# Eight output stores at the end of a fused linear-attention and MLP kernel, issued by SyncE instead of GpSimd and ScalarE

## The chip, the cores and the metric

The kernel runs on one core of one Trainium2 chip. The metric is the device time of one execution in microseconds. Before the change it was 406.97 us as the median of three runs (405.87, 406.97 and 407.54).

## What is computed

The kernel computes a residual sum of a linear-attention block and an MLP with squared ReLU, both on the layer-normalised input, for 2048 tokens of 512 channels, in float32:

```python
phi = lambda t: jnp.where(t > 0, t + 1, jnp.exp(t)) + 1e-6
q, k, v = split_heads(xn @ wqkv)             # 32 heads of 16
kv = einsum("bhsd,bhse->bhde", phi(k), v); z = einsum("bhsd->bhd", phi(k))
A = (phi(q) kv / (phi(q) z + 1e-6)) @ wo
h = xn @ w1 + b1                             # 512 x 1376
B = relu(h)**2 @ w2 + b2                     # 1376 x 512
out = x + A + B                              # xn = layernorm(x)
```

(The split into heads and the einsums are shortened here.)

## The kernel before

Tokens stand in four groups of 512 (`BT`); a group is four tiles of 128 rows. A float32 product is made of three passes over high and low parts (`PASSES`, line 134). A first phase goes over all tokens for keys and values; then the groups 3 and 2 are done up to their stores, and then the groups 1 and 0 (`t1`, `t2` in the last part of the code). Instructions are issued to each engine in the order in which the code stands (`manual_schedule`, line 75): each engine works through its own list in order, and waits at an instruction until what it needs is there. A DMA is such an instruction too: the engine that issues it waits first for the data, then hands the transfer over, and goes on.

The change is at the very end, in the second product of the groups 1 and 0. That product is made block by block: the rows are the two token groups (r = 0 is group 1, r = 1 is group 0), the columns the left and the right half of the 512 output channels (`LO`, `HI`). Seven products M1 to M7 on TensorE make the four blocks, in the tiles `res[r, half]`; each such tile starts as the residual input (`load_block`, line 1732) and gets its products by `into` (line 1767), as an accumulating DMA from GpSimd or as an addition on VectorE.

- Block (0,0) is stored by line 1947, block (1,1) by line 1971: four stores each, issued by SyncE. A store of a block (`store_block`, line 1738) is cut by channel group; each of the four moves 128 KB in pieces of 256 bytes.
- Block (0,1) lacks its last product. It goes by four stores of SyncE into a scratch tensor `rowsd` (line 1965), and comes back by one load of 512 KB, issued by GpSimd, with tokens on the partitions, as `rows` (line 1967).
- Block (1,0) is turned out of the bank `d` by VectorE (`M4t`, line 1973), added into `res10` (lines 1974 and 1773) and stored by line 1975.
- Last, TensorE makes the product M3 for group 1 in four banks `end`, one for each tile of 128 tokens (line 1980, by the helper at line 140). When a bank is done, VectorE adds it into `rows` (line 1982), and a store of 128 KB writes that tile's right half (line 1984).

The counters that the rows of the order below name (`DMAHW0` to `DMAHW7` for transfers of SyncE and ScalarE, `DMASW0` to `DMASW7` for those of GpSimd) count transfers that have landed; they are used in turn, and a DMA that takes a counter waits until the transfer that had it before has landed. At the end of the program (line 2008) SyncE waits for all counters, and then all engines meet.

Of the kernel before, what the change touches and what calls it, by code (L numbers as in the profile page):

```python
# [13 lines left out]
P = 128  # L14
# [4 lines left out]
def kernel(  # L19
# [30 lines left out]
    nc = tc.nc  # L50
    xf = x.rearrange("b s d -> (b s) d")
    of = out.rearrange("b s d -> (b s) d")
# [84 lines left out]
    def three(ps, a, b, first, last):  # L137

        for n, (u, v) in enumerate(PASSES):
            nc.tensor.matmul(ps, lhsT=a[u], rhs=b[v], start=first and n == 0, stop=last and n == 2)  # L140
# [440 lines left out]
    for k in range(1, NJ):  # L581
        rows = slice(32 * k, 32 * (k + 1))
# [3 lines left out]
    for i0 in range(0, NT, TB):  # L586
# [6 lines left out]
        if i0 < NPE:  # L593
            single = work.tile([P, 3, 512], F32, name=f"xg{i0}s", tag="r0")
            for k in range(3):
                i = i0 + k - 1
# [3 lines left out]
        for k in range(0, n, 2):  # L600
            i = i0 + TB - n + k
# [401 lines left out]
    LO, HI = slice(0, D // 2), slice(D // 2, D)  # L1003
# [185 lines left out]
    for p in range(NO + 1):  # L1189
        at_p = AT[p]  # L1190
        kind, k = order[p] if p < NO else ("", 0)
        fa, fb = 2 * k, 2 * k + 1

        was, k = order[p - 1] if p else ("", 0)
# [481 lines left out]
    def rights(name, part):  # L1676

        key, kind, r, at = RIGHT[name]
        if part == "q":
            return [[(m if kind == "m" else mt)[u][:, 2 * r + i, at] for u in range(2)] for i in range(2)]  # L1680
        return [part_at[key, k] for k in ((0, 1), (2, 3), (4,))[part]]
# [39 lines left out]
    def token_rows(r, half, g, x):  # L1721

        t = (t2 if r else t1) * BT
        return rows_of(x[t:t + BT, half * 256:(half + 1) * 256], g)

    def rows_of(x, g):
        return x.rearrange("(b r) (g c) -> g r b c", r=Q, g=NJ)[g]

    def res_rows(o, g):
        return o[Q * g:Q * (g + 1)].rearrange("p a n -> p (a n)").rearrange("p (b c) -> p b c", c=2 * Q)  # L1730
# [7 lines left out]
    def store_block(r, half, to=None, engs=(nc.sync,)):  # L1738
        for g in range(NJ):
            o = token_rows(r, half, g, of) if to is None else rows_of(to, g)  # L1740
            engs[g % len(engs)].dma_start(o, res_rows(res[r, half], g))
# [25 lines left out]
    def into(r, half, tiles, eng="dma"):  # L1767
        for u in range(2):
            o = res[r, half][:, u]
            if eng == "dma":  # L1770
                nc.gpsimd.dma_start(o, tiles[u], accum_op=OP.add)
            else:
                nc.vector.tensor_tensor(out=o, in0=tiles[u], in1=o, op=OP.add)
# [64 lines left out]
    for p in range(NO):  # L1838
        kind, k = order[p]
# [126 lines left out]
    rows = work.tile([P, TB, 256], F32, name="rows", tag="x1")  # L1966
# [5 lines left out]
    do(low, 2)  # L1972
    m4 = turned_out("M4", Dc)
    into(1, 0, m4, "dve")
    store_block(1, 0, engs=(nc.gpsimd,))
    for parts in ((0, 1), (2, "q")):
        chunks = [(a, b) for part in parts for a, b in zip(half_units["M3", part], rights("M3", part))]
        for k in range(TB):
            for n, (a, b) in enumerate(chunks):
                three(ends[k], [v[:, k * P:(k + 1) * P] for v in a], b, False, "q" in parts and n == len(chunks) - 1)  # L1980
            if "q" in parts:
                nc.vector.tensor_tensor(out=rows[:, k], in0=ends[k], in1=rows[:, k], op=OP.add)
                i = t1 * TB + k
                nc.scalar.dma_start(of[i * P:(i + 1) * P, HI], rows[:, k])


# [26 lines left out]
```

## Time and profile before

| what | value |
|---|---|
| runs shown | 405.87, 406.97, 407.54 us |
| the profiled execution's own time | 406.98 us |
| its span | 404.9 us |
| mean granted clock of TensorE | 0.996 |
| output stores of SyncE from `res` at line 1741 | 8, of 128 KB |
| output stores of GpSimd from `res10` | 4, of 128 KB |
| output stores of ScalarE from `rows` | 4, of 128 KB |
| software queue of GpSimd | 4016 packets, 9.45 MB, 12.7% of the DMA engines' span |
| hardware queue of SyncE | 73472 packets, 77.23 MB, 61.0% |
| hardware queue of ScalarE | 656 packets, 0.52 MB, 0.4% |

The span is what the profile covers, from the first instruction to the last; the time of the execution is 2.08 us longer. In the rows of the profile the engines are PE (TensorE; PEld is its weight load), DVE (VectorE), ACT (ScalarE), POOL (GpSimd) and SP (SyncE); a name with a q behind it (SPq, ACTq, POOLq) is the engine's instruction queue, where DMAs are issued and waits are held. Times are in us from the span's start.

### The profile page before, as it was taken

How to read it: one execution, taken by the hardware profiler on the slowest of the kernel's cores; microseconds unless marked ns; L12 is line 12 of the kernel's file. 1: busy time of each engine (PE TensorE's matmuls, PEld its weight loads, DVE VectorE, ACT ScalarE, POOL GpSimd, SP SyncE). 2: the span in 40 equal slices, each digit the busy share in tenths (PEclk: the TensorE clock that was granted, in tenths of full speed). 3: DMA queues.
4: the chain of work that ended last, by engine and by line, in shares of the span. 5: the costliest groups of instructions: out<-in, count | busy, mean ns of one | idle time of the engine just before them, and what ended most of it. 6: DMA issues, size and time to landing. Idle time of an engine off the chain costs nothing.

```text
span 404.9 us, 5834 instructions
## 1 busy us (share of the span) xinstructions
PE 395.6 (98%) x1940; PEld 327.1 (81%) x1940; DVE 318.4 (79%) x537; ACT 259.8 (64%) x434; POOL 66.0 (16%) x106
## 2 busy tenths in 40 slices
PE   8999999999999999999999999999999999999992
PEld 7788888888788888888878888888888788888892
DVE  5886667587898989988499997269999895987841
ACT  5677777556788689887727860565986784565400
POOL 5443333220410000030000300200000001231111
PEclk9999999999999999999999999999999999999998
DMA  7857647911698745799796974896796867999953
GB/s 212 279 164 228 210 155 208 259 29 26 235 358 285 274 150 184 264 285 334 237 410 207 188 206 137 290 291 196 222 287 196 295 202 157 218 182 195 181 121 91
DMA packets 78172, 87.55 MB, mean 216 GB/s; under 512 B 24256, under 2 KB 59200, under 8 KB 77376
## 3 DMA queue, kind: packets, MB, share of 16 engines
q1 hardware_dynamic: 73472, 77.23, 61.0%
q0 software_dynamic: 4016, 9.45, 12.7%
q10 hardware_dynamic: 656, 0.52, 0.4%
q8 instruction: 15, 0.25, 0.3%
q14 instruction: 13, 0.11, 0.1%
HBM read 52.05 MB, written 28.84 MB: 200 GB/s over the span
## 4 chain that ended last, share of the span: by engine, by line
PE 93%; issue 3%; DVE 1%; DMA 1%; POOL 0%; ACT 0%; POOLq 0%
PE b L528 22%; PE acc L140 19%; PE pk L384 11%; PE kx L404 11%; PE a L1697 7%; PE b_c L528 5%; PE b_a L528 4%; PE b L1697 2%; PE y L1697 2%; PE d L1697 2%; PE b_b L528 2%; PE pz L140 1%; PE acc L539 1%; DMA x<-in_A_x_dram 1%; PE b L140 1%
## 5 line engine op out<-in xcount | busy, mean ns | idle before, releaser
L140 PE MATMUL acc<-w2r,s 128*128 128x512 f32 x240 | 57.0, 391 | 0.0
L140 PEld LDWEIGHTS acc<-w2r,s 128*128 128x128 f32 x240 | 44.9, 188 | 9.9 <-issue 0.4
L404 PE MATMUL kx<-pk,tok 128*128 128x512 f32 x192 | 46.0, 390 | 0.0
L404 PEld LDWEIGHTS kx<-pk,tok 128*128 128x128 f32 x192 | 36.0, 188 | 7.6 <-ACT pk L121 0.2
L528 PE MATMUL b<-T,aop 128*128 128x512 f32 x168 | 41.8, 390 | 0.0
L528 PEld LDWEIGHTS b<-T,aop 128*128 128x128 f32 x168 | 31.4, 188 | 7.4 <-ACT t L121 0.8
L365 POOL TENSOR_TENSOR tok<-xp,tok 128x512 fp32r<-128x512 f32 x15 | 20.2, 1344 | 39.8 <-ACT tok L121 39.8
L1088 POOL DMA_DIRECT2D res<-in_B_b_dram x8 | 7.1, 1004 | 107.7 <-DVE S L766 59.5
L132 DVE TENSOR_TENSOR M<-h,M 128x1024 fp32r<-128x1024 f32 (+1 forms) x15 | 15.2, 1038 | 5.4 <-ACT M L121 5.4
L1630 POOL DMA_DIRECT2D h<-h x6 | 5.3, 924 | 85.5 <-issue 64.5
L121 ACT ACTIVATE T<-Tf 128x512 fp32r<-128x512 f32 x16 | 9.4, 623 | 15.0 <-DVE Tf L709 14.9
L528 PE MATMUL b<-xs0h,aop 128*128 128x512 f32 x56 | 18.6, 392 | 0.0
L121 ACT ACTIVATE M<-h 128x1024 fp32r<-128x1024 f32 (+1 forms) x15 | 13.2, 908 | 7.6 <-PE a L1697 2.8
L121 ACT ACTIVATE pk<-k 128x512 fp32r<-128x512 f32 x16 | 10.1, 630 | 9.1 <-DVE k L379 9.1
L375 ACT ACTIVATE k<-pk 128x512 f32<-128x512 f32 x16 | 9.4, 589 | 9.8 <-PE pk L384 9.8
L140 PE MATMUL acc<-mh,aTsr 128*128 128x512 f32 x48 | 15.6, 390 | 0.0
L392 DVE SCALAR_TENSOR_TENSOR pk<-k,pk 128x512 fp32r<-128x512 f32 x16 | 11.3, 708 | 4.3 <-ACT pk L121 3.4
L242 DVE BATCH_NORM_STATS2 st<-x 128x6 f32<-128x512 f32 x16 | 10.9, 684 | 4.2 <-DMA x<-in_A_x_dram 4.1
L132 DVE TENSOR_TENSOR w2r<-r,w2r 128x512 fp32r<-128x512 f32 (+2 forms) x20 | 13.7, 683 | 0.5 <-ACT w2r L121 0.4
L379 DVE SCALAR_TENSOR_TENSOR k<-pk,k 128x512 f32<-128x512 f32 x16 | 10.9, 679 | 3.4 <-ACT k L377 3.0
L384 PE MATMUL pk<-wkh,xs1h 128*128 128x512 f32 x32 | 12.7, 396 | 0.2 <-ACT xs1h L332 0.2
L384 PE MATMUL pk<-wkl,xs0h 128*128 128x512 f32 x32 | 12.5, 390 | 0.0
(399 smaller groups left out, 1065.4 us busy)
## 6 DMA issues: line engine op xcount, KB each, us to landing
r<-in_B_w_dram SPq DMA_DIRECT2D x26, 256.0 KB, 4.4
aop_0d<-aop SPq DMA_DIRECT2D x7, 512.0 KB, 4.3
aop_1d<-aop SPq DMA_DIRECT2D x7, 512.0 KB, 5.4
aop_2d<-aop SPq DMA_DIRECT2D x7, 512.0 KB, 5.7
via<-xp SPq DMA_DIRECT2D x5, 512.0 KB, 2.7
xg<-via SPq DMA_DIRECT2D x20, 128.0 KB, 2.8
xTd<-t SPq DMA_DIRECT2D x8, 256.0 KB, 4.0
x<-in_A_x_dram SPq DMA_DIRECT2D x4, 512.0 KB, 4.5
```

Of the source, the lines that this page charges most:

```text
L121: nc.scalar.activation(o, i, AF.Copy, bias=bias)
L132: nc.vector.tensor_tensor(out=l, in0=src, in1=f32(h), op=OP.subtract)
L140: nc.tensor.matmul(ps, lhsT=a[u], rhs=b[v], start=first and n == 0, stop=last and n == 2)
L242: nc.vector.bn_stats(st[:, k, :], xr[tiles[k]])
L365: ENG[el].tensor_tensor(out=l, in0=src, in1=f32(h), op=OP.subtract)
L375: nc.scalar.activation(p, ps, AF.Relu, scale=-1.0)
L379: nc.vector.scalar_tensor_tensor(p, ps, 0.0, p, op0=OP.max, op1=OP.add)
L384: nc.tensor.matmul(ps, lhsT=cols(i)[u][:, j, slot(i)], rhs=w[v][:, j, :], start=first and n == 0, stop=last and n == len(steps) - 1)
L392: nc.vector.scalar_tensor_tensor(pk[i][:, 1], p, 1e-6, f32(pk[i][:, 0]), op0=OP.add, op1=OP.subtract)
L404: nc.tensor.matmul(kxp[c], lhsT=tok[i][:, u, c * P:(c + 1) * P], rhs=pk[i][:, v], start=i == 0 and (u, v) == first, stop=i == NT - 1 and ( ...
L528: nc.tensor.matmul(ps, lhsT=a[u][:, j * P:(j + 1) * P], rhs=b[v][:, j, :], start=first and j == 0 and n == 0, stop=last and j == 1 and n == 2,
L1697: nc.tensor.matmul(ps[e], lhsT=w, rhs=a[v], start=first and c == n == 0, stop=False, skip_group_check=True)
```

## The change

Two lines change. The four stores of block (1,0) lose the argument that gave them to GpSimd, so they take the default of `store_block`, SyncE; the four stores of `rows` are issued by SyncE in place of ScalarE. No data, size, address or computation changes, and no line changes its place.

```diff
@@ -1972,7 +1972,7 @@
     do(low, 2)
     m4 = turned_out("M4", Dc)
     into(1, 0, m4, "dve")
-    store_block(1, 0, engs=(nc.gpsimd,))
+    store_block(1, 0)
     for parts in ((0, 1), (2, "q")):
@@ -1981,7 +1981,7 @@
             if "q" in parts:
                 nc.vector.tensor_tensor(out=rows[:, k], in0=ends[k], in1=rows[:, k], op=OP.add)
                 i = t1 * TB + k
-                nc.scalar.dma_start(of[i * P:(i + 1) * P, HI], rows[:, k])
+                nc.sync.dma_start(of[i * P:(i + 1) * P, HI], rows[:, k])
```

SyncE's list at its end, with what each DMA waits for (`res_3537` is block (1,1), `res_3450` block (1,0), a minus is before and a plus after the change):

```order
 L1741 DMA out_dram<-res_3537 32x16x64 [waits DMAHW6_49]
-L1741 DMA out_dram<-res_3537 32x16x64 [waits DMAHW1_49]
-L1741 DMA out_dram<-res_3537 32x16x64 [waits DMAHW4_49]
+L1741 DMA out_dram<-res_3537 32x16x64 [waits DMAHW7_49]
+L1741 DMA out_dram<-res_3537 32x16x64 [waits DMAHW0_49]
+L1741 DMA out_dram<-res_3450 32x16x64 [waits DMAHW1_49,DVE_49]
+L1741 DMA out_dram<-res_3450 32x16x64 [waits DMAHW2_49]
+L1741 DMA out_dram<-res_3450 32x16x64 [waits DMAHW3_49]
+L1741 DMA out_dram<-res_3450 32x16x64 [waits DMAHW4_49]
+L1984 DMA out_dram<-rows 128x256 [waits DMAHW5_49,DMASW0_49,DVE_49]
+L1984 DMA out_dram<-rows 128x256 [waits DMAHW6_49,DVE_49]
+L1984 DMA out_dram<-rows 128x256 [waits DMAHW7_49,DVE_49]
```

The row of the fourth store of `rows` reads like the last one, with `DMAHW0`. SyncE gets eight DMAs behind its former last one, and the last two stores of block (1,1) take other counters.

GpSimd's list at its end, where `rows<-rowsd` is the load of the scratch tensor:

```order
 L1771 DMA res_3537<-Yt_3652 128x512 [waits DVE_49]
 L1967 DMA rows<-rowsd 128x4x256 [waits DMAHW2_49,DMAHW3_49,DMAHW1_49,DMAHW4_49,DMASW0_49,Activation_49]
-L1741 DMA out_dram<-res_3450 32x16x64 [waits DMASW1_49,DVE_49]
-L1741 DMA out_dram<-res_3450 32x16x64 [waits DMASW2_49]
-L1741 DMA out_dram<-res_3450 32x16x64 [waits DMASW3_49]
-L1741 DMA out_dram<-res_3450 32x16x64 [waits DMASW4_49]
 L2008 UNCONDITIONAL_BRANCH
```

The load of `rows` becomes GpSimd's last DMA, and it is issued behind the same waits.

ScalarE's list at its end, behind its last two copies:

```order
 L121 ACTIVATE M_3749<-h_2667 128x512 [waits DMASW0_49]
 L121 ACTIVATE M_q<-q_2571 128x1024 [waits DMASW1_49,DVE_49,PE_49]
-L1984 DMA out_dram<-rows 128x256 [waits DMAHW7_49,DMASW0_49,DVE_49]
-L1984 DMA out_dram<-rows 128x256 [waits DMAHW0_49,DVE_49]
-L1984 DMA out_dram<-rows 128x256 [waits DMAHW2_49,DVE_49]
-L1984 DMA out_dram<-rows 128x256 [waits DMAHW3_49,DVE_49]
 L2008 UNCONDITIONAL_BRANCH
```

Nothing stood behind these stores on ScalarE but the end of the program. TensorE's and VectorE's lists are unchanged.

## The prediction

> **What bounds the kernel now.** I read the page first, for the engine that fills the span, then the chain of waits over the last 30 us, since the change touches only the end of the program.
>
> ```profile
> span 404.9 us, 5834 instructions
> PE 395.6 (98%) x1940; PEld 327.1 (81%) x1940; DVE 318.4 (79%) x537; ACT 259.8 (64%) x434; POOL 66.0 (16%) x106
> PE   8999999999999999999999999999999999999992
> ```
>
> TensorE is busy for 98% of the span, in every one of the 40 slices but the last, where it is busy for two tenths. A slice is 404.9/40 = 10.1 us, so some 8 us at the end run without TensorE. That is the stretch in which the moved stores lie. The chain of waits, with start, length and holder:
>
> ```profile
> 374.73 9.54 PE d L1697 x42
> ...
> 386.52 1.44 DVE M4t L1762 x4
> 387.96 1.19 DVE res L1773 x2
> 389.15 2.93 issue
> 392.08 0.69 POOL out_dram L1741
> 392.76 2.19 issue
> 394.95 0.66 POOL out_dram L1741
> 395.62 2.71 issue
> 398.32 0.65 POOL out_dram L1741
> 398.97 2.15 issue
> 401.12 0.68 POOLq L2008
> ```
>
> The chain leaves TensorE when bank `d` is done, passes VectorE's turning and adding of block (1,0), and from 389.15 to the end it is GpSimd alone: four stores, each with 0.65 to 0.69 us of its own and 2.2 to 2.9 us of "issue" ahead of it, a time in which GpSimd waits for nothing that the profile shows. The data of all four were there at 389.15, yet the last store was issued only at 401.14. Its start to start distances are 2.87, 3.37 and 2.82 us. The other work of this stretch, from the timeline:
>
> ```profile
> 383.76 3.14 SPq L1741 DMA_DIRECT2D out_dram<-res  x4
> 387.33 0.80 POOL L1967 DMA_DIRECT2D rows<-rowsd  x1 [10.03 <-DMA rowsd<-res]
> 392.08 0.69 POOL L1741 DMA_DIRECT2D out_dram<-res  x1 [3.95 <-issue]
> 394.38 3.52 ACTq L1984 DMA_DIRECT2D out_dram<-rows  x4
> 396.79 0.28 PE L140 MATMUL end<-mh,M_q 128*128 128x256 f32 x1
> 397.11 0.42 DVE L1982 TENSOR_TENSOR rows<-end,rows 128x256 f32<-128x256 f32 x1 [0.64 <-PE end L140]
> 401.14 0.66 POOL L1741 DMA_DIRECT2D out_dram<-res  x1 [2.17 <-issue]
> ```
>
> TensorE ends at 397.07, VectorE's fourth addition at 397.53, and ScalarE's fourth store is issued at once: the four take 394.38 to 397.90, with 0.34 us for the last, so it starts at 397.56. SyncE has issued its last DMA by 386.90. So the end is bound neither by TensorE nor by the transfers themselves but by how slowly GpSimd puts out four stores. The windows of 1 us show this from the DMA side (the last two numbers are the busy share of the 16 DMA engines, and GB/s):
>
> ```profile
> 392.00:393.00 1.00, 1.00 (x10) 1.00 (x10) 0.00 (x0) 0.00 (x0) 0.69 (x1) 1.00 0.00 0
> 393.00:394.00 1.00, 1.00 (x11) 1.00 (x10) 0.07 (x1) 0.00 (x0) 0.00 (x0) 1.00 0.75 131
> 401.00:402.00 1.00, 0.00 (x0) 0.00 (x0) 0.00 (x0) 0.00 (x0) 0.66 (x1) 0.75 0.00 0
> 402.00:403.00 1.00, 0.00 (x0) 0.00 (x0) 0.00 (x0) 0.00 (x0) 0.00 (x0) 0.50 0.75 131
> ```
>
> One store of 128 KB keeps the DMA engines busy for about 0.75 us, and they stand idle between two of them.
>
> **The change part by part.** First, the four stores of block (1,0). What goes is GpSimd's tail from 389.15. What comes is four issues on SyncE, which can start when the additions end, at 389.15 + 0.03. How long SyncE takes for such stores, and how long they and the other transfers need from issue to landing:
>
> ```profile
> L1741 SPq DMA_DIRECT2D out_dram<-res x8: 316/567/1593, 377.8 to 386.6; - x8
> DMA to landing us min/median/max: 2.3/2.9/3.9
> ...
> rows<-rowsd POOLq DMA_DIRECT2D x1, 512.0 KB, 4.4
> out_dram<-res POOLq DMA_DIRECT2D x1, 128.0 KB, 2.5
> out_dram<-rows ACTq DMA_DIRECT2D x1, 128.0 KB, 1.7
> ...
> DMA to landing us min/median/max: 1.7/1.9/2.9
> ```
>
> (The first two rows are those of line 1741, the landing over all its stores; the next two are the load of `rows` and GpSimd's last store, then ScalarE's last store alone, and the last row is that of all four stores of line 1984.) Four stores of the same form took SyncE 3.14 us above, so the last is issued by about 392.3, and with the longest landing of 3.9 us it has landed by 396.2. That lies beside TensorE's last product, which runs to 397.07: it costs nothing. If that cover were gone, these stores would still end 7.4 us earlier than GpSimd's last did (401.14 + 2.5 = 403.64).
>
> The counters cost nothing either. The four new stores take `DMAHW1` to `DMAHW4`, last held by the four stores into `rowsd`; GpSimd's load at 387.33 waited for just these, so they had landed. The stores of `rows` take the counters of block (1,1), whose last issue was at 386.6 and landed by 386.6 + 3.9 = 390.5 at worst, ahead of the first addition's end at 394.35. The two stores of block (1,1) that change counters now wait for stores of block (0,0), which went out ahead of those into `rowsd`; should that cost some tenths, SyncE's idle time from 386.90 to 389.15 covers it.
>
> Second, the four stores of `rows`. They are queued behind block (1,0) on SyncE, done by 392.3, and the first is due at 394.38, so SyncE stands waiting for VectorE as ScalarE did. The last starts at 397.56 as before. What a store of this form takes from SyncE to landing the trace doesn't show; the same transfer from ScalarE took 1.7 us with nothing beside it, and 2.9 at worst, when GpSimd's stores ran beside it. SyncE's own stores, of 256-byte pieces, took 2.3 to 3.9. I take 1.7, since it is the same transfer and at 397.56 nothing else is left to move, and keep 1.7 to 2.9.
>
> Third, traffic: the new stores meet the load of `rows`, which landed at 387.33 + 4.4 = 391.7. The first addition needs it at 393.93, so there are 2.2 us to spare, and since the four additions take 4 x 0.42 = 1.7 us together, the last one would be late only if the load landed after 397.53 - 1.7 = 395.8, 4.1 us later than it did. I cost this at nothing; four stores at 0.75 us of engine time make 3.0 us in all.
>
> Fourth, the end of the program. SyncE waits there for the counters in turn:
>
> ```profile
> SPq L2008 <- DMA out_dram<-res: 5.3, 1, 5.3
> ...
> L2008 SPq DRAIN x3: 7/7/7, 404.1 to 404.4; - x3
> L2008 POOLq DRAIN x3: 46/98/2639, 401.1 to 404.7; - x3
> ```
>
> Its last long wait, 5.3 us, was for GpSimd's stores. From the last landing (403.64) to the span's end (404.9) are 1.26 us, of which the part behind SyncE's drain at 404.1 is 0.8 and the rest goes over counters that had long landed. I keep the 1.26 us, and take 0.46 us less as the low end. GpSimd's drain, 2.64 us from 401.1, moves ahead to its load of `rows` and is hidden.
>
> **The sum.** The new last landing is 397.56 + 1.7 = 399.26, in place of 403.64; with 1.26 us behind it the span ends at 400.5 in place of 404.9, 4.4 us earlier. Against the profiled execution's 406.98, which agrees with the median of the runs (406.97), this is **402.6 us**, 1.1% faster. What is late next is TensorE's last product: from there on, VectorE's addition, one store and the program's end follow in a chain that nothing else shares.
>
> The Trainium skill ("DMA: Bandwidth & Descriptors", section "Issuing engines are not separate DMA queues") says that DMAs of the scalar, sync and gpsimd engines run on the same 16 DMA engines, and that issuing from several only saves issue time, "usually small relative to the DMA itself". By that rule alone this change would move little. The trace differs for GpSimd: 2.8 to 3.4 us from issue to issue against 0.75 us of DMA time.
>
> **The rivals.** The first, on the other side: **SyncE's single list becomes the bound**. Eight stores now go through one engine in order, and an issue can be slow: 1.59 us was the longest of its block stores above, and elsewhere in the trace
>
> ```profile
> 360.00 11.69 SPq L1736 DMA_DIRECT2D res<-in_A_x_dram  x12
> 204.02 6.67 SPq L1121 DMA_DIRECT2D w2sd<-w2t  x3
> ```
>
> The loads of the blocks took 0.97 us each with the DMA engines full, the larger stores of line 1121 2.2 us each. With x us per issue the eighth starts at 389.18 + 7x. The forecast holds while that is ahead of 397.56, x up to 1.20; the end is where it was when it reaches 403.64 - 1.7 = 401.94, x = 1.82; beyond that the change is slower. At 2.2 the eighth starts at 404.6, the span ends at 404.6 + 1.7 + 1.26 = 407.5, and the time is **409.6 us**. Against it: stores of the same size and form took 0.67 to 0.79 us each, and four of the eight are spread by VectorE over 3.2 us. A case between, all at 1.59, puts the eighth at 400.3 and gives **405.4 us**, within 0.5%.
>
> The Trainium skill ("Perfetto Trace Analysis", section "DMA Optimizations") advises to balance DMAs across sync, scalar and GPSIMD where descriptor generation is the bottleneck; this change takes them together on one, and by that page it would be this rival. The trace bears it out only for GpSimd, the engine that it empties.
>
> Second: **the last store lands slower from SyncE**, with the block's stores still draining ahead of it on the same queue. At the 2.9 us of the worst store of `rows` the end moves by 1.2, to **403.8 us**. For it: SyncE's own rows have 2.3 as their least. Against: these are 512 pieces of 256 bytes each, and the block's stores should have landed 1.4 us ahead.
>
> Third: **the change doesn't shorten the end**, since the load of `rows` is held up by the new stores until about 400.2; the additions then end at 401.9, the last store lands at 403.6, and the time stays at **407.0 us**. That asks for 8.5 us of delay from four stores of 0.75 us.
>
> **How the numbers follow.** A measurement of this kernel can tell about 0.5% (2.03 us) from no change, so faster means below 404.9. The forecast has 0.84, the slower landing 0.08, the case between on SyncE's list 0.03, the held load 0.02, and SyncE's list as the bound, with more than 409.0, 0.03. The first two are faster, 0.92, and a part of the case between adds 0.02: 0.94. Within 0.5% lie the rest of it and the held load, 0.03. The range goes from the forecast less the 0.46 us at the end and about half the spread of the runs shown (407.54 - 405.87 = 1.67, half 0.8, of which I take 0.5), 401.6, up to the slower landing with the same 0.5, 404.3.
>
> **What would show it.** In the changed kernel's chain of waits no row of GpSimd should stand behind the load of `rows`; the end should read TensorE `end`, VectorE `rows`, SyncE's store of line 1984. SyncE's four stores of block (1,0) should start at about 389.2 and take 2.6 to 3.2 us; its last store should start 0.03 us behind VectorE's last addition, at about 397.6, and land 1.7 us later; from TensorE's last matmul to the span's end, 404.9 - 397.07 = 7.8 us before, there should be 3.4 us. The forecast is wrong if SyncE's issues take over 1.2 us each, if the additions wait for the load of `rows` in place of TensorE, or if the program's end has a part that GpSimd's stores had covered.

## The result, and the profile after

The changed kernel took 403.31 us as the median of five runs (402.91 to 403.62), against 406.97 us (405.87 to 407.92) for the kernel before: 3.7 us less, a ratio of 0.9908 with a 95% interval of 0.9888 to 0.9929. The forecast was 402.6 us, the range 401.6 to 404.3. The profiled execution has a span of 401.2 us in place of 404.9.

The page of the changed kernel, with the same rows as before and the queues of GpSimd (q0) and ScalarE (q10):

```profile
span 401.2 us, 5834 instructions
PE 395.2 (98%) x1940; PEld 326.6 (81%) x1940; DVE 318.1 (79%) x537; ACT 259.6 (65%) x434; POOL 63.0 (16%) x102
PE   7999999999999999999999999999999999999996
q0 software_dynamic: 3824, 8.92, 12.7%
q10 hardware_dynamic: 80, 0.00, 0.0%
```

TensorE's busy time is nearly what it was, 395.2 us in place of 395.6; what went is time without it, and the last slice shows six tenths in place of two. ScalarE's queue has lost its 0.52 MB, and GpSimd's 0.53 MB. The chain of waits at the end:

```profile
375.00 9.52 PE d L1697 x42
...
387.34 10.01 PE end L140 x84
397.35 0.02 issue
397.37 0.42 DVE rows L1982
```

GpSimd is gone from it. The chain now stays on TensorE through its last product into the banks `end`, and ends on VectorE's fourth addition at 397.80. The timeline of the issuing queues:

```profile
389.43 2.11 SPq L1741 DMA_DIRECT2D out_dram<-res  x4
394.65 3.51 SPq L1984 DMA_DIRECT2D out_dram<-rows  x4
```

SyncE puts out block (1,0) in 2.11 us, from 389.43 on, where GpSimd had taken from 392.08 to 401.80. Then it stands waiting until the first tile of `rows` is ready. The stores of `rows` by themselves, and the program's end (line 2008):

```profile
L1984 SPq DMA_DIRECT2D out_dram<-rows x4: 332/342/357, 394.6 to 397.8; - x4
DMA to landing us min/median/max: 1.7/1.7/1.7
...
L2008 SPq EVENT_SEMAPHORE  x11: 17/28/28, 398.2 to 401.2; - x11
L2008 POOLq DRAIN  x3: 46/98/4760, 387.4 to 401.0; - x3
L2008 SPq DRAIN  x3: 7/7/7, 400.4 to 400.7; - x3
```

The last store starts at 397.83, 0.03 us behind VectorE, and lands 1.7 us later, at 399.5, as the prediction had it. But from there SyncE needs until 400.41 to come through its list of counters to its drain (the row behind the last counter), 0.89 us; before, it had been 0.43 (403.67 to 404.10). From SyncE's drain to the span's end it is 0.83 us in both.

### The profile page after: what moved, and what is told of

It reads as the page before. It is cut to its first block, busy times and chain, and to the rows that moved or that the text cites. A ratio compares the mean times of both kernels' runs of the same rounds, so it can differ in the third digit from the quotient of the medians.

```text
span 401.2 us, 5834 instructions
## 1 busy us (share of the span) xinstructions
PE 395.2 (98%) x1940; PEld 326.6 (81%) x1940; DVE 318.1 (79%) x537; ACT 259.6 (65%) x434; POOL 63.0 (16%) x102
## 4 chain that ended last, share of the span: by engine, by line
PE 97%; DMA 1%; ACT 0%; SPq 0%; DVE 0%; issue 0%
PE b L528 22%; PE acc L140 19%; PE pk L384 11%; PE kx L404 11%; PE a L1697 7%; PE b_c L528 5%; PE b_a L528 4%; PE end L140 2%; PE b L1697 2%; PE y L1697 2%; PE d L1697 2%; PE b_b L528 2%; PE pz L140 1%; DMA rk<-in_A_wqkv_dram 1%; PE acc L539 1%; PE b L140 1%
## 5 line engine op out<-in xcount | busy, mean ns | idle before, releaser
L384 PE MATMUL pk<-wkh,xs0h 128*128 128x512 f32 x32 | 12.4, 389 | 0.0
```

The costliest lines, as they stand in the source:

```text
L384: nc.tensor.matmul(ps, lhsT=cols(i)[u][:, j, slot(i)], rhs=w[v][:, j, :], start=first and n == 0, stop=last and n == len(steps) - 1)
```

## The experiments

The main theory was that GpSimd sets the end by putting out its four stores one at a time. Its rivals: the stores of `rows` brought part of the gain; the load ahead of them on GpSimd held the stores; SyncE's single list is a new bound. From the changed profile came a second question: why SyncE's way through its last list had become longer. A ratio is always to the kernel before, run beside the one in question.

**Block (1,0) back on GpSimd.**

```diff
-    store_block(1, 0)
+    store_block(1, 0, engs=(nc.gpsimd,))
```

> The four stores of block (1,0) go back to GpSimd; the four stores of rows stay on SyncE. Theory (the end is set by GpSimd putting out its four stores one by one, 2.8 to 3.4 us from start to start): all of the gain goes, last GpSimd store issued at about 401, span about 404.9, time about 407.0, ratio to before 1.00. Rival (the move of the stores of rows from ScalarE brought part of the gain): the time stays visibly under 407, 405 or less if it brought half.

Measured: 407.13 us, ratio 1.0006 (0.9993 to 1.0018). The chain of waits is that of before:

```profile
388.98 3.02 issue
392.00 0.69 POOL out_dram L1741
392.68 2.21 issue
394.89 0.66 POOL out_dram L1741
395.55 2.76 issue
398.32 0.65 POOL out_dram L1741
398.97 2.18 issue
401.15 0.68 POOLq L2008
```

All of the gain goes, with the stores of `rows` still on SyncE. The first line of the change carries it.

**The stores of `rows` back on ScalarE.**

```diff
-                nc.sync.dma_start(of[i * P:(i + 1) * P, HI], rows[:, k])
+                nc.scalar.dma_start(of[i * P:(i + 1) * P, HI], rows[:, k])
```

> The four stores of rows go back to ScalarE; block (1,0) stays on SyncE. Theory: the whole gain stays, last store issued by ScalarE about 0.03 us behind VectorE's last addition and landed 1.7 us later, time 403.0 to 403.6 as after the change. Rival (the stores of rows matter): the gain goes in part, 405 or more.

Measured: 403.36 us, ratio 0.9914 (0.9901 to 0.9927). The number is the expected one, the way to it is not. SyncE's queue, its waits, and the landing of ScalarE's stores of line 1984:

```profile
389.20 8.32 SPq L1741 DMA_DIRECT2D out_dram<-res  x4
...
396.15 1.36 SPq L1741 DMA_DIRECT2D out_dram<-res  x2
...
SPq L1741 <- DMA out_dram<-rows: 6.8, 2, 6.1
...
DMA to landing us min/median/max: 1.7/2.0/2.6
```

Two of SyncE's four stores of block (1,0) were held until 396.15 and later, for 6.1 us the first of them. In this arrangement they take the counters `DMAHW7` and `DMAHW0`, which stores of `rows` on ScalarE hold, and wait for those to land, although no data ask for it. So they ran into ScalarE's last store, which took 2.6 us to land in place of 1.7, at 400.16. SyncE's list behind it was shorter (0.33 us to its drain in place of 0.89), so the two kernels come out alike by chance. A cleaner arrangement comes below.

**Only the load of `rows` moved, from the kernel before.**

```diff
-    nc.gpsimd.dma_start(rows, rowsd.rearrange("(k p) n -> p k n", p=P))
+    nc.sync.dma_start(rows, rowsd.rearrange("(k p) n -> p k n", p=P))
```

> The kernel before the change, with only the 512 KB load of rows from the scratch tensor issued by SyncE in place of GpSimd, so that GpSimd has nothing but the four stores at the end. Theory (each store takes GpSimd about 2.9 us by itself): the stores start at about 389.2 in place of 392.1 and keep their distance, the fourth is issued at 398.3 and lands at 400.8, span about 402.1, time about 404.1, ratio 0.993. Rival (the load held GpSimd, and behind nothing it puts out stores quickly, at the 0.7 us of their own rows): the stores are out by 392, and the time is that after the change, 403.3.

Measured: 405.01 us (404.19 to 407.07), ratio 0.9955 (0.9940 to 0.9969); the profiled execution took 404.56 with a span of 402.5.

```profile
389.58 0.72 POOL L1741 DMA_DIRECT2D out_dram<-res  x1 [13.01 <-DVE res L1773]
392.79 0.67 POOL L1741 DMA_DIRECT2D out_dram<-res  x1 [2.50 <-issue]
395.67 0.66 POOL L1741 DMA_DIRECT2D out_dram<-res  x1 [2.21 <-issue]
398.80 0.65 POOL L1741 DMA_DIRECT2D out_dram<-res  x1 [2.47 <-issue]
```

With nothing ahead of them the stores begin 2.5 us earlier and keep their distance of 2.9 to 3.2 us. So the load had held the first one, and each store costs GpSimd about 3 us by itself. The median is 0.9 us over what was expected; the first store went 0.5 us behind its data, and the rest lies in the spread of these runs.

**Three of the four stores on GpSimd.**

```diff
-    store_block(1, 0)
+    store_block(1, 0, engs=(nc.sync, nc.gpsimd, nc.gpsimd, nc.gpsimd))
```

> The changed kernel with three of the four stores of block (1,0) on GpSimd, one on SyncE. Theory: the third GpSimd store is issued at about 398.3 and lands at 400.8, 1.3 to 1.5 us behind the last store of rows (399.5); the time is 404.3 to 404.8, which lies between the two kernels, 2.3 to 2.9 us (one store) under the kernel before. Rival (GpSimd costs once for its queue at the end, not per store): as the kernel before, 407.

Measured: 404.48 us, ratio 0.9945 (0.9931 to 0.9958). The third and last GpSimd store went out at 397.91:

```profile
394.77 0.66 POOL L1741 DMA_DIRECT2D out_dram<-res  x1 [2.20 <-issue]
397.91 0.65 POOL L1741 DMA_DIRECT2D out_dram<-res  x1 [2.48 <-issue]
```

The cost is per store: one store less on GpSimd, 2.4 us less (406.85 beside it for the kernel before). By the traces the last GpSimd store went out 3.2 us earlier, and 0.4 us of that was lost again behind its landing: from there to the span's end it is 1.66 us in place of 1.26. The section on the prediction says where this comes from.

**One store on GpSimd, three on SyncE.**

```diff
-    store_block(1, 0)
+    store_block(1, 0, engs=(nc.sync, nc.sync, nc.sync, nc.gpsimd))
```

> The changed kernel with one of the four stores of block (1,0) on GpSimd, three on SyncE. GpSimd's one store is issued at about 392 and landed by 395, ahead of the last store of rows, so by the theory of the issue distance the time is that after the change, 403.3. It also moves the counter of the last store of rows from DMAHW0 to DMAHW7, which SyncE's list at the end of the program asks for last but for one row. Theory of the end's list (behind the last landing SyncE still steps over the counters that come later in its list, some 0.06 us each, and in the changed kernel one step took 0.37 us): from the last landing to the span's end 1.7 us become about 0.9, the time 402.5 to 402.9. Rival (the 0.37 us step and the list are hidden, or the end waits for something else): no change, 403.3.

Measured: 402.15 us (402.12 to 402.49), ratio 0.9883 (0.9866 to 0.9899). This is faster than the changed kernel. The stores of line 1984 and SyncE's drain:

```profile
L1984 SPq DMA_DIRECT2D out_dram<-rows x4: 332/341/357, 394.3 to 397.4; - x4
DMA to landing us min/median/max: 1.7/1.7/1.7
...
L2008 SPq DRAIN  x3: 7/7/7, 399.2 to 399.5; - x3
```

The last store starts at 397.45 and has landed at 399.15; SyncE drains at 399.23, 0.08 us later in place of 0.89. The span ends 0.92 us behind the last landing in place of 1.72.

**The same counter, with all stores on SyncE.** So that the store on GpSimd is not the reason, the changed kernel got one DMA less on SyncE far ahead of the end:

```diff
-                nc.sync.dma_start(b1s[a:a + n, NF - 1:], b1[o:o + n, None])
+                (nc.sync if a else nc.gpsimd).dma_start(b1s[a:a + n, NF - 1:], b1[o:o + n, None])
```

> The changed kernel with one load of 64 values of b1, far ahead of the end, issued by GpSimd in place of SyncE. All sixteen stores stay as in the changed kernel, but SyncE has one DMA less and the last store of rows takes the counter DMAHW7, the last in SyncE's list at the program's end, in place of DMAHW0, second in it. Theory of the end's list: from the last landing to the span's end 0.9 us in place of 1.7, time 402.2 to 402.7, as with one store on GpSimd (402.15). Rival (GpSimd's one store, which relieves SyncE's queue, made that kernel faster): the time is that after the change, 403.3.

Measured: 402.21 us (402.08 to 402.54), ratio 0.9879 (0.9860 to 0.9899).

```profile
L2008 SPq EVENT_SEMAPHORE  x11: 17/28/28, 397.9 to 400.1; - x11
L2008 POOLq EVENT_SEMAPHORE  x4: 17/17/17, 399.4 to 400.0; - x4
L2008 POOLq DRAIN  x3: 46/98/4722, 387.9 to 399.9; - x3
L2008 SPq DRAIN  x3: 7/7/7, 399.3 to 399.6; - x3
```

The last store lands at 399.22 and SyncE drains at 399.31. The theory of the list holds: the engines, the order and the data at the end are those of the changed kernel, and only the counters have moved on by one. On the same chip, the changed kernel and the kernel with one store on GpSimd were run once more.

> The changed kernel as it is, on the same chip as the others of this call: 403.3.

> The kernel with one store of block (1,0) on GpSimd and three on SyncE once more, beside the changed kernel: 402.2, about 1.1 us under it.

Measured: 403.01 us (402.85 to 403.23) and 402.11 us (401.78 to 402.47), so 0.9 us between them. 402.1 to 402.2 us is the lowest time of these experiments.

**The stores of `rows` on ScalarE without the crossed counters.**

```diff
-    store_block(1, 0)
+    store_block(1, 0, engs=(nc.sync, nc.gpsimd))
...
-                nc.sync.dma_start(of[i * P:(i + 1) * P, HI], rows[:, k])
+                nc.scalar.dma_start(of[i * P:(i + 1) * P, HI], rows[:, k])
```

> The four stores of rows on ScalarE again, block (1,0) half on SyncE and half on GpSimd, so that SyncE's two stores take counters that no store of rows holds and can go at 389.2 (in the run with all four on SyncE two of them waited until 396 and 397 for the stores of rows). Theory (which engine issues the stores of rows makes no difference; only what else lands beside them and the end's list do): last store of rows issued 0.03 us behind VectorE's addition and landed 1.7 us later, four counters left in the list behind it, 1.1 to 1.2 us to the end, time 402.3 to 402.8. Rival (stores of rows from ScalarE land slower than from SyncE): 403 or more.

Measured: 402.81 us (401.95 to 403.56), ratio 0.9892 (0.9876 to 0.9909), at the upper end of what was expected.

```profile
389.51 0.85 SPq L1741 DMA_DIRECT2D out_dram<-res  x2
392.33 0.69 POOL L1741 DMA_DIRECT2D out_dram<-res  x1 [3.83 <-issue]
394.73 3.52 ACTq L1984 DMA_DIRECT2D out_dram<-rows  x4
395.21 0.66 POOL L1741 DMA_DIRECT2D out_dram<-res  x1 [2.20 <-issue]
...
L2008 SPq DRAIN  x3: 7/7/7, 400.0 to 400.3; - x3
```

SyncE's two stores go at once. ScalarE's last store starts at 397.91, lands 1.74 us later, and 1.15 us lead from there to the end with four rows of counters left. With the block's stores all but landed (the last at 398.08), ScalarE's last store lands no slower than SyncE's; in this one execution VectorE's fourth addition came 0.4 us later (397.88) than in the two faster kernels (397.42 and 397.49). The six runs lie so far apart that their median by itself doesn't settle it against 403.

**The stores of `rows` on GpSimd.**

```diff
-                nc.sync.dma_start(of[i * P:(i + 1) * P, HI], rows[:, k])
+                nc.gpsimd.dma_start(of[i * P:(i + 1) * P, HI], rows[:, k])
```

> The changed kernel with the four stores of rows on GpSimd (128 pieces of 1 KB each), block (1,0) on SyncE. Theory (GpSimd's time goes with the pieces of a store, 512 against 128): the four stores keep pace with VectorE, the last is issued at about 397.8 and lands some 2.0 to 2.5 us later in place of 1.7, so that the time is 403.6 to 404.2. Rival (GpSimd takes about 2.9 us for any store): the four stores are spread over 394.7 to 403.4, land at about 405.5, time about 409.

Measured: 403.07 us, ratio 0.9905 (0.9890 to 0.9920). The stores, and their landing:

```profile
395.63 0.55 POOL L1984 DMA_DIRECT2D out_dram<-rows  x1 [0.54 <-DVE rows L1982]
396.64 0.54 POOL L1984 DMA_DIRECT2D out_dram<-rows  x1 [0.47 <-DVE rows L1982]
397.75 0.54 POOL L1984 DMA_DIRECT2D out_dram<-rows  x1 [0.57 <-DVE rows L1982]
...
DMA to landing us min/median/max: 2.0/2.0/2.0
```

Here GpSimd waits for VectorE before each store and keeps its pace of 1.06 us. So GpSimd is slow with the 512 pieces of 256 bytes of a block's store, not with a store as such: 128 pieces of 1 KB, the same 128 KB, cost it 1.1 us at most. Whether it is the number of the pieces or their form is not separated here; they change together. The time came 0.5 us under what was expected, since SyncE's list behind the last landing took 0.42 us and not the 0.89 on which that was built.

**Block (1,0) cut into sixteen stores on SyncE.** `store_block` got a number of cuts, four for this block; nothing else was changed.

```diff
-            engs[g % len(engs)].dma_start(o, res_rows(res[r, half], g))
+            n = 16 // cuts
+            for b in range(0, 16, n):
+                engs[g % len(engs)].dma_start(o[:, b:b + n], res_rows(res[r, half], g)[:, b:b + n])
```

> The changed kernel with each of the four stores of block (1,0) cut into four, so that SyncE issues sixteen DMAs of 32 KB there in place of four of 128 KB, and the four stores of rows behind them. Rival of the prediction (SyncE's single list becomes the bound): at 0.6 us for each issue whatever its size the sixteen end at about 399, the four stores of rows follow to about 400.5, and the time rises by 2.5 to 3 us to about 406. Theory that an issue's time goes with its pieces (128 in place of 512, about 0.15 to 0.35 us each): the sixteen end by about 395, VectorE still sets the last store, time 403.3. Both hold the counters, which after eight issues wait for landings.

Measured: 402.89 us (402.56 to 403.75), ratio 0.9902 (0.9886 to 0.9917). SyncE's queue and VectorE's last addition (two lines further down in this kernel):

```profile
388.48 7.43 SPq L1743 DMA_DIRECT2D out_dram<-res  x16
396.33 1.82 SPq L1986 DMA_DIRECT2D out_dram<-rows  x4
...
397.03 0.42 DVE L1984 TENSOR_TENSOR rows<-end,rows 128x256 f32<-128x256 f32 x1 [0.63 <-PE end L140]
```

Sixteen DMAs took 7.43 us, 0.46 each, between the two expectations: with a quarter of the pieces an issue costs hardly less than the 0.53 us (2.11/4) of a whole store. Now SyncE is late: the first store of `rows` starts at 396.33 in place of some 394.3, and the last 0.3 us behind the addition (397.75 against 397.45). But the sixteen were out by 395.91, and between SyncE's next row, at 395.96, and the first store of `rows` lies a single step of 0.37 us; the changed kernel has the same step in its list at the end, as the next section tells. By an estimate from these rows, with a step of 0.06 us that store would have gone at about 396.0, and at the pace of these four (0.47 us) the last at about 397.45, with VectorE's addition. So even twenty DMAs in place of eight bring SyncE's list only to the edge of being the bound; the 0.3 us are worth as much as that step, and a shorter list at the end (0.26 us from the last landing to the drain) more than pays for them.

## Why the prediction was right, and where a term was off

**What bounded the end** was read rightly. Block (1,0) on GpSimd gives back the whole gain (1.0006), one store less on GpSimd lets its last one go 3.2 us earlier, and moving the load alone shows that the distance belongs to the stores.

**Block (1,0) on SyncE costs nothing**, as forecast: out by 391.54 and covered by TensorE's product to 397.3. The forecast had 392.3.

**The last store** landed 1.7 us after its issue, at the low end of the bounds of 1.7 to 2.9. The block's stores had landed by 394.15, and only the end of the store of `rows` ahead of it (to 398.46) ran beside it. The rival of a slower landing, 403.8 us, didn't come; its mechanism is seen in the second experiment, where two stores did run beside the last one and it took 2.6.

**SyncE's single list** did not become the bound: 0.53 us per issue for the block and 0.33 to 0.36 for the stores of `rows`, far from the 1.20 from which it would have cost anything. **The load of `rows`** landed 4.5 us after its issue, in place of 4.4.

**The end of the program** is the term that was mis-sized. The prediction kept its 1.26 us from the last landing to the span's end, with 0.46 less as the low end. It became 1.72, so from TensorE's last matmul to the span's end it is 3.9 us and not the 3.4 forecast. With the 0.27 us by which VectorE's last addition came later in this execution (397.80 against 397.53, on the same lists of TensorE and VectorE; in all thirteen traces it lies between 397.09 and 397.88), that is the 0.7 us between the forecast of 400.5 for the span's end and the 401.2 measured. One of the prediction's own signs of being wrong, a part of the program's end that had not shown before, so came true in part; it was not GpSimd's stores that had covered it. The prediction saw that the list takes time but took its length to be fixed. It goes with the place in the list of the counter that lands last, and with one long step. The rows of SyncE's list (each asks for two counters) in the traces:

| kernel | last landing, us | counters' rows left behind it | to SyncE's drain, us |
|---|---|---|---|
| one store on GpSimd | 399.15 | 0 | 0.08 |
| counter moved, all on SyncE | 399.22 | 0 | 0.09 |
| sixteen cuts | 399.54 | 3 | 0.26 |
| `rows` on ScalarE, clean | 399.65 | 4 | 0.32 |
| before | 403.67 | 6 | 0.43 |
| `rows` on GpSimd | 399.74 | 6 | 0.42 |
| three stores on GpSimd | 400.44 | 5 | 0.71 |
| after | 399.52 | 7 | 0.89 |

Without the last two kernels of the table, each row left costs 0.06 us. The changed kernel has 7 left, one more than the kernel before, which makes 0.06 of the 0.46 us. The larger part, 0.3 us, is a single step of 0.37 us in place of 0.06; the remaining 0.1 lies in rows that took 0.07 to 0.09. The three stores on GpSimd show a step of the same size.

The step stands at SyncE's 464th instruction, in all eight traces whose list is that long (466 to 484 instructions) and whatever that instruction is: a row of counters in the changed kernel, the drain with three stores on GpSimd, the first store of `rows` with sixteen cuts. The lists of the other five end earlier, at 458 (the kernel before) to 463, and they have no such step at the end. So the move of eight stores to SyncE made its list longer than 463 and brought the step in; with the first line of the change alone (`rows` on ScalarE) it is 463 and the step is missing. With one store on GpSimd and with the moved counter the step is there too, but SyncE makes it while the last store is still on its way, and it is hidden.

Why it is there stays open. What the traces add: 128 instructions earlier, at the 336th, all thirteen show a step of the same size (0.36 to 0.38 us), and 0.6 to 0.9 us behind the 464th a transfer of 8 KB goes over the queue q14, which the profile calls "instruction"; in the five shorter lists no such transfer comes at the end before the span is over. That points to the loading of SyncE's list and not to the counters, but no run changed that alone.

The second line of the change, the stores of `rows` on SyncE, gives no time by itself: with block (1,0) on GpSimd the time is that of before (1.0006), and from ScalarE with free counters the last store lands as fast. It keeps SyncE's stores of the block from waiting for ScalarE's counters, and it takes SyncE's list past the step; neither was foreseen.

## What to carry to other kernels

Where the last rows of a chain of waits are DMA issues of GpSimd with "issue" gaps between them, count the pieces of each transfer: stores in 512 pieces went out at 3 us each from GpSimd and at 0.53 us from SyncE. Then follow the counters as well as the data: two engines that share counters can wait for each other without any need, and the end of a program costs a step for each row of counters that is asked for behind the last one to land. Which counter the last store takes was worth 0.8 us here (403.01 against 402.21 us): seven rows, and the long step among them. And a DMA moved to an engine adds to that engine's list even where nothing waits for it.

## What was not expected of the hardware

- GpSimd's time for a store went with its form: 2.8 to 3.4 us for 512 pieces of 256 bytes, at most 1.1 us for 128 pieces of 1 KB, both 128 KB.
- SyncE's time hardly did: 0.46 us for 128 pieces of 256 bytes, 0.53 us for 512 of them.
- A store of 128 KB in pieces of 1 KB landed 1.7 us after its issue from SyncE or ScalarE and 2.0 us after it from GpSimd.
- SyncE steps over a row of counters that have landed in 0.06 us at the program's end, but takes 0.37 us to its 464th instruction, in each of the eight traces that have one.
